# A fused H3 layer and gated product, forward and backward: the product of gate and up on GpSimd, part of the gradient turned by DMA, two buffers for k and v, paced late weights

## The chip, the cores and the metric

One core of one Trainium2 chip. The metric is the device time of one execution in microseconds (us). Every ratio below is between fast runs of the same chip and the same rounds. A time of a stage comes from one profiled run of each kernel, some of them on other chips; kernels with the same code in a stage differ there by up to some 5 us, so smaller differences of one stage are not read as effects, except where several runs agree. A ratio is the mean time of one kernel's fast runs over the mean of the other's in the same rounds, so it is not quite the ratio of the medians quoted beside it.

TensorE is PE in the profile, VectorE DVE, ScalarE ACT, GpSimd POOL, SyncE SP.

## The reference, cut to what matters

Forward pass and all gradients in bfloat16, with S = 2048 rows, D = 1024, F = 3584:

```python
xn = layernorm(q)
k_shift = causal 4-tap filter of k with shift_k;  kv = k_shift * v
y  = irfft(rfft(kv, 2S) * rfft(ssm_k, 2S))[:S] + kv * ssm_D      # long convolution
g  = xn @ w_gate;  u = xn @ w_up;  h = g * u                     # 2048 x 3584
out = q + (xn * y) * silu(h @ w_down)
# returned: out and the gradients of q, k, v, shift_k, ssm_k, ssm_D, w_gate, w_up, w_down
```

The product h = g * u is the one that the change moves. `dbm`, the gradient that flows into `h @ w_down`, is the one that it turns by DMA.

## The kernel before: the parts that the change touches

Stage one runs the projections of gate and up on TensorE in 14 slabs of 256 columns of F, and beside them, as generators that hand over in turn, the forward convolution, whose arithmetic is almost all on VectorE. `tt` is a VectorE `tensor_tensor`, `V` is `nc.vector`; `st` stores through GpSimd's DMA queue, `ld` loads or stores through SyncE's.

```python
def gu_unit(sl, b0, n, w, tick):                      # n row blocks of one slab
    gut = fg.tile([P, 4, 2, SLW], BF16, name="gut")
    hN = fg.tile([P, 4, SLW], BF16, name="hN")
    for i in range(n):
        ...                                           # 8 matmuls into ps
        nc.scalar.copy(out=gut[:, i]..., in_=ps[:])
        tick()                                        # convolution work is handed out here
    sta(GUd[...], gut[:, 0:n])
    tt(hN[:, 0:n], gut[:, 0:n, 0], gut[:, 0:n, 1], MUL)          # h on VectorE
    st(Hd[sl][:, b0:b0 + n, :], hN[:, 0:n])
    def turn():                                       # TensorE transposes of hN, some units later
        ...
    defer(turn)

# forward convolution
def load_kv(dp, c):
    v = U[4][:, 0:2048]...;  cld_v(v, c, dp * 256, 256)
    k = kst.tile([P, 2, 11, P], BF16, name="k")       # one buffer
    ...
def shift(dp):                                        # per piece: 7 products and sums, then
    ...
    st(KSHd[...], acc)
    nx = 2 * dp + c + 1                               # the next piece
    if nx < 8: load_kv(nx // 2, nx % 2)
...
w, wld = load_slab(sl, nc.sync)
if sl in (2, 4, 7):
    with tc.issue_after(wld.ins):
        copy_k({2: 1, 4: 2, 7: 3}[sl])                # k to its layout in DRAM, for the loads of k

# down product with the gate: 16 row blocks b
st(DBMd[:, b, :], dbm)
def turn():                                           # 8 transposes a block on TensorE
    ...
defer(turn)

# gradient of w_down, slab k
if k in (1, 2, 3, 4, 5): load_wgu(k - 1, ...)         # transposing loads for the last stage
if k in (6, 7, 8, 9): ts.append(load_dgut(0, k - 6))
...
ld(o_dwd[f0:f0 + P, :], wbs)
```

## Time and profile before

The time before was 2076.62 us (median of 3 runs). The stages below are cut at the first matmul of each stage in the trace of the profiled run; the last one ends with the last instruction of an engine, so they add up to the span within a few us.

| stage | us | TensorE waits most for |
|---|---|---|
| projections and forward convolution | 572.1 | hN (product on VectorE), 15.5 us |
| down product and gate | 204.8 | nothing for more than 1.1 us at a time |
| gradients of gate and up, backward convolution | 660.2 | dht (copies on ScalarE), 12.8 us; kvx, which the change is after, 4.2 us |
| gradient of w_down | 219.5 | h, 6.1 us |
| input gradient | 412.9 | dxn, 2.4 us |

### The profile page before, as it was taken

To read this page: it belongs to the slowest core of one execution; us is meant where nothing else is said; L and a number is where in the kernel's file an instruction comes from. 1 tells how busy PE (TensorE), PEld (TensorE's weight loads), DVE (VectorE), ACT (ScalarE), POOL (GpSimd) and SP (SyncE) were. 2 spreads that over 40 slices of the span, in tenths; PEclk is the share of its full clock that TensorE was granted. 3 is DMA by queue.
4 is the path that set the end of the run, shared out by engine and by line. 5 is a ranking of instruction groups with operands and counts; after the bars stand their busy time and mean duration, and the time that the engine had idled before them with its cause. 6 is when DMAs were issued, how large, how long until landed. Compare 5 with 4: busy or idle time off the path is not lost.

```text
span 2072.6 us, 29102 instructions
## 1 busy us (share of the span) xinstructions
PE 1974.6 (95%) x11626; PEld 1060.4 (51%) x11626; DVE 1488.6 (72%) x2009; ACT 617.7 (30%) x966; POOL 342.9 (17%) x499
## 2 busy tenths in 40 slices
PE   6989999999999998999898999999989999999998
PEld 3445555555544446666565555565444444444443
DVE  8689999999745556887799999989488024444343
ACT  5644544444423332222222222222122201101112
POOL 3212212221112111000122112011111101110100
PEclk9999999999999999999999999999999999999999
DMA  8675776567597869666888888668974989393921
GB/s 286 221 261 202 241 246 241 198 220 264 184 329 253 278 238 291 215 201 183 265 260 244 238 243 259 202 228 235 188 228 155 230 198 226 98 203 98 232 73 56
DMA packets 454792, 451.30 MB, mean 218 GB/s; under 512 B 237072, under 2 KB 381240, under 8 KB 440192
## 3 DMA queue, kind: packets, MB, share of 16 engines
q1 hardware_dynamic: 310320, 186.94, 35.4%
q0 software_dynamic: 45200, 189.08, 26.6%
q10 hardware_dynamic: 99136, 73.42, 11.7%
q8 instruction: 91, 1.49, 0.3%
q14 instruction: 45, 0.37, 0.1%
HBM read 208.15 MB, written 194.02 MB: 194 GB/s over the span
## 4 chain that ended last, share of the span: by engine, by line
PE 56%; DVE 19%; issue 14%; DMA 8%; POOL 2%; ACT 1%; SPq 1%; ACTq 0%; POOLq 0%; DVEq 0%
PE psx L1213 17%; PE psb L1092 10%; PE psbm L954 8%; PE psb L1190 7%; DVE W L199 5%; PE psg L553 5%; DVE m L199 5%; PE psb L1073 4%; DVE HX L199 2%; DMA B<-KFd 2%; DVE U L199 1%; DMA KSLd<-in_A_k_dram 1%; DMA B<-HFd 1%; DVE KX L199 1%; PE psY L404 1%
## 5 line engine op out<-in xcount | busy, mean ns | idle before, releaser
L553 PE MATMUL psg<-wslab,U 128*128 128x512 bf16 x1792 | 414.9, 382 | 7.1 <-ACT U L529 5.0
L1092 PE MATMUL psb<-U,U 128*128 128x512 bf16 x1792 | 396.9, 380 | 7.1 <-ACT dht L1075 3.3
L1213 PE MATMUL psx<-U,dgut 128*128 128x512 bf16 x1536 | 335.7, 379 | 2.4 <-DVE dxn L199 2.4
L1213 PEld LDWEIGHTS <-dgut 128*128 128x128 bf16 x1792 | 174.0, 98 | 213.3 <-issue 6.0
L1092 PEld LDWEIGHTS <-U 128*128 128x128 bf16 x1792 | 175.3, 98 | 209.8 <-issue 10.4
L553 PEld LDWEIGHTS <-U 128*128 128x128 bf16 x1792 | 173.6, 99 | 192.1 <-issue 7.3
L1073 PE MATMUL psb<-wdt,U 128*128 128x256 bf16 x1792 | 206.3, 276 | 10.7 <-ACT dht L1075 9.5
L1190 PE MATMUL psb<-U,U 128*128 128x512 bf16 x896 | 201.2, 386 | 10.9 <-DMA U<-Hd 6.1
L555 ACT CAST gut<-psg 128x512 bf16<-128x512 f32 x224 | 131.0, 585 | 227.6 <-PE psg L553 215.7
L1073 PEld LDWEIGHTS <-U 128*128 128x128 bf16 x1792 | 176.9, 99 | 35.7 <-issue 11.3
L954 PE MATMUL psbm<-U,ht 128*128 128x512 bf16 x784 | 171.8, 379 | 0.3 <-DMA ht<-HTd 0.3
L1096 ACT CAST wb<-psb 128x512 bf16<-128x512 f32 x112 | 65.5, 585 | 319.3 <-PE psb L1092 224.2
L199 DVE TENSOR_TENSOR m<-A,B 128x1024 bf16<-128x1024 bf16 (+1 forms) x160 | 116.7, 792 | 47.8 <-DMA B<-KFd 32.2
L1190 PEld LDWEIGHTS <-U 128*128 128x128 bf16 x896 | 88.3, 99 | 117.2 <-issue 11.7
L199 DVE TENSOR_TENSOR W<-W 128x1024 f32<-128x1024 f32 (+1 forms) x144 | 146.0, 1032 | 2.7
L199 DVE TENSOR_TENSOR dka<-dkh,Wbc 128x1024 bf16<-128x1024 bf16 x16 | 11.1, 692 | 165.8 <-DMA dkh<-DKSHd 165.8
L954 PEld LDWEIGHTS <-ht 128*128 128x128 bf16 x784 | 76.0, 98 | 89.5 <-DMA ht<-HTd 0.8
L1236 ACT ACTIVATE dx_t<-dxn 128x1024 bf16<-128x1024 f32 (+1 forms) x17 | 17.1, 1007 | 341.6 <-DVE dxn L199 290.2
L1075 ACT CAST dht<-psb 128x512 bf16<-128x512 f32 x112 | 65.2, 587 | 154.9 <-PE psb L1073 102.4
L1192 ACT CAST wbs<-psb 128x512 bf16<-128x512 f32 x56 | 32.7, 585 | 176.1 <-PE psb L1190 140.5
L199 DVE TENSOR_TENSOR W<-W,psP 128x512 f32<-128x512 f32 x128 | 80.7, 681 | 5.8 <-ACT W L229 5.8
L199 DVE TENSOR_TENSOR U<-U,dht 128x2048 bf16<-128x2048 bf16 x56 | 69.1, 1233 | 21.4 <-ACT dht L1075 21.4
(233 smaller groups left out, 2362.2 us busy)
## 6 DMA issues: line engine op xcount, KB each, us to landing
U<-GUd SPq DMA_DIRECT2D x28, 1024.0 KB, 7.5
DGd<-U ACTq DMA_DIRECT2D x56, 512.0 KB, 4.9
GUd<-gut ACTq DMA_DIRECT2D x54, 512.0 KB, 4.6
A<-DYFd POOLq DMA_DIRECT2D x16, 1024.0 KB, 8.0
U<-Hd SPq DMA_DIRECT2D x15, 1024.0 KB, 6.1
out_dram<-wb ACTq DMA_DIRECT2D x224, 64.0 KB, 3.1
Hd<-hN POOLq DMA_DIRECT2D x54, 256.0 KB, 3.5
HTd<-hT POOLq DMA_DIRECT2D x54, 256.0 KB, 3.4
```

The source lines that it names most:

```text
L199: V.tensor_tensor(o, a, b, op)
L404: nc.tensor.matmul(ps[:, i, :], TI[:, j, r, k, :], gseg(G, r, j, k), start=(n == 0), stop=(n == 3))
L553: gu_mm[0] = nc.tensor.matmul(ps[:], XNT[q][:, dc, qi * P:(qi + 1) * P], w[:, dc].rearrange("p a f -> p (a f)"), start=(dc == 0), stop=(dc ...
L555: nc.scalar.copy(out=gut[:, i].rearrange("p a f -> p (a f)"), in_=ps[:])
L954: nc.tensor.matmul(ps[:, dh * 512:(dh + 1) * 512], ht(fc)[:, i * P:(i + 1) * P], WD[fc // 4][:, fc % 4, dh * 512:(dh + 1) * 512], start=(f ...
L1073: nc.tensor.matmul(ps[:, x * SLW:(x + 1) * SLW], DBMT[2 * hf + g][:, dc, (b % 4) * P:(b % 4 + 1) * P], wdt[:, dc, :], start=(dc == 0), sto ...
L1075: nc.scalar.copy(out=dht[:, 2 * e:2 * e + 2].rearrange("p b f -> p (b f)"), in_=ps[:])
L1092: nc.tensor.matmul(ps[:], XN[b // 4][:, b % 4, dc * P:(dc + 1) * P], dgus[b // 8][:, b % 8].rearrange("p a f -> p (a f)"), start=(b == 0), ...
L1096: nc.scalar.copy(out=wb[:].rearrange("p a f -> p (a f)"), in_=ps[:])
L1190: nc.tensor.matmul(ps[:], h[:, b, f * P:(f + 1) * P], DBM[b // 4][:, b % 4, dh * 512:(dh + 1) * 512], start=(b == 0), stop=(b == NB - 1))
L1192: nc.scalar.copy(out=wbs[:, dh * 512:(dh + 1) * 512], in_=ps[:])
L1213: nc.tensor.matmul(ps[:, dh * 512:(dh + 1) * 512], t[n][:, f, i * P:(i + 1) * P], WGU[n][:, f, dh * 512:(dh + 1) * 512], start=(n == 0 and ...
```

## The change

The intent was to relieve VectorE, the second bound of stage one, of the 60 products hN, and TensorE of 96 transposes, and to take away waits for k, for kvx and for slabs of h behind late weights. The diff, cut to its core (a fixed alternation of ScalarE and VectorE for some copies in the layer norm, the order of one root, and the layout of DBMd that the transposing loads need are left out):

```diff
-    nc.vector.tensor_tensor(diag[:], ident_f[:, 0:64], ident_f[:, 64:128], ADD)      # moved later
@@ gu_unit
-        tt(hN[:, 0:n], gut[:, 0:n, 0], gut[:, 0:n, 1], MUL)
+        nc.gpsimd.tensor_tensor(hN[:, 0:n], gut[:, 0:n, 0], gut[:, 0:n, 1], MUL)
@@ load_kv, shift
-            v = U[4][:, 0:2048].rearrange("p (a x) -> p a x", a=8)
+            v = U[4][:, 2048 * c:2048 * c + 2048].rearrange("p (a x) -> p a x", a=8)
-            k = kst.tile([P, 2, 11, P], BF16, name="k")
+            k = kst.tile([P, 2, 11, P], BF16, name="k", bufs=2)
-                nx = 2 * dp + c + 1
+                nx = 2 * dp + c + 2
+        load_kv(0, 1)
@@ dy_forward: load kv before dy
@@ down product
-        defer(turn)
+        if b >= 12:
+            defer(turn)
+        if bp in (3, 5, 7):
+            q = (bp - 3) // 2
+            with tc.issue_after(ht_ld.ins):
+                nc.sync.dma_start_transpose(out=DBMT[q], in_=DBMd[512 * q:512 * q + 512, :])
@@ backward pump, two ticks later
-        bpump((bcnt[0] - 8) / (BT - 8))
+        bpump((bcnt[0] - 10) / (BT - 10))
@@ gradient of w_down
-        if k in (1, 2, 3, 4, 5):
-            load_wgu(k - 1, u8((7, 8, 9, 10, 2)[k - 1], a=4))
-        if k in (6, 7, 8, 9):
-            ts.append(load_dgut(0, k - 6))
+        with tc.issue_after(wst.ins) if k > 0 else nullcontext():
+            if k in (1, 2, 3, 4, 5):
+                load_wgu(k - 1, u8((7, 8, 9, 10, 2)[k - 1], a=4))
+            if k in (6, 7, 8, 9):
+                ts.append(load_dgut(0, k - 6))
-            ld(o_dwd[f0:f0 + P, :], wbs)
+            wst = ld(o_dwd[f0:f0 + P, :], wbs)
```

More of the change, by code (lines that the diff above doesn't have):

```diff
@@ L1 @@
-from contextlib import ExitStack
+from contextlib import ExitStack, nullcontext
 import numpy as np
@@ L92, in build_kernel @@
     DXNAd = dram.tile([P, NB, D], BF16, name="DXNAd")
-    DBMd = dram.tile([P, NB, D], BF16, name="DBMd")
+    DBMd = dram.tile([S, D], BF16, name="DBMd")
     KSHd = dram.tile([8, P, NB, P], BF16, name="KSHd")
@@ L486, in ln_load @@
         ld(x4[:, 0:n, :], xq[:, c, r0:r0 + n, :])
-    tr_ln = [None]
+    tr_ln, act_copy = [None], [None]
     def layer_norm(b0, n, x4):
@@ L503, in layer_norm @@
         r0_ = small("r0_")
-        root = nc.scalar.activation(r0_, vpe, ACT.Sqrt)
+        with tc.issue_after(act_copy[0].ins) if act_copy[0] is not None else nullcontext():
+            root = nc.scalar.activation(r0_, vpe, ACT.Sqrt)
         mean_b = small("mean_b", BF16)
@@ L528, in layer_norm @@
                 tr_ln[0] = nc.tensor.transpose(ps[:, dc, :], x4[:, i, dc * P:(dc + 1) * P], ident[:])
-            nc.any.tensor_copy(XNT[q][:, :, qi * P:(qi + 1) * P], ps[:])
+            if i % 2 == 0:
+                act_copy[0] = nc.scalar.copy(out=XNT[q][:, :, qi * P:(qi + 1) * P], in_=ps[:])
+            else:
+                V.tensor_copy(XNT[q][:, :, qi * P:(qi + 1) * P], ps[:])
         return last, root, st(XNd[:, b0:b0 + n, :], x4[:, 0:n, :])
@@ L707, in build_kernel @@
                 build_tables(ps_st, tg, ang)
+    tt(diag[:], ident_f[:, 0:64], ident_f[:, 64:128], ADD)
     for p_ in (lnp, lns, tg, bsb):
@@ L775, in load @@
         def load(ds):
+            kv = cx.tile([P, NB, P], BF16, name="kvx")
+            cld(kv[:], KVd[ds])
             x = cx.tile([P, NB, P], BF16, name="dyx")
             cld(x[:], DYd[ds])
-            kv = cx.tile([P, NB, P], BF16, name="kvx")
-            cld(kv[:], KVd[ds])
             return x, kv
@@ L979, in gate @@
         tt(dbm, dgg, sig, MUL)
-        st(DBMd[:, b, :], dbm)
+        st(DBMd[b * P:(b + 1) * P, :], dbm)
         tt(ds_t, do_t, gg, MUL)
@@ L1129, in build_kernel @@
             for q in range(4):
-                ld(DBM[q], DBMd[:, 4 * q:4 * q + 4, :])
+                ld(DBM[q], DBMd[512 * q:512 * q + 512, :].rearrange("(b u) d -> u b d", u=P))
             hs[1] = load_h(1, HSL[1])
```

## The prediction

> **What bounds the kernel now.** I read the page first, then busy time by stage, then the waits of TensorE (PE), then the timelines at the longest waits. The stages are: projections of gate and up with the forward convolution between them (60 to 575 us), the down product with the gate (575 to 776), the gradients of gate and up with the backward convolution (776 to 1437), the weight gradient of down (1437 to 1650), the input gradient (1650 to the end).
>
> ```profile
> PE   6989999999999998999898999999989999999998
> DVE  8689999999745556887799999989488024444343
> ```
>
> PE is busy nearly everywhere, VectorE (DVE) only in stage one and from 1000 to 1300 us. In us, with instruction counts in brackets, for PE, PEld, DVE, ACT and POOL:
>
> ```profile
> 60.00:575.00 515.00, 490.94 (x3048) 273.80 (x3047) 465.11 (x608) 247.43 (x386) 117.99 (x179) 0.99 0.68 232
> 1000.00:1300.00 300.00, 278.82 (x1699) 167.90 (x1698) 292.54 (x345) 71.67 (x127) 56.47 (x85) 0.98 0.83 245
> 1437.00:1650.00 213.00, 202.12 (x1032) 95.30 (x1031) 130.85 (x151) 41.97 (x75) 28.12 (x18) 0.97 0.86 203
> ```
>
> Stage one has two bounds at once: PE 491 and DVE 465 of 515 us. What PE cannot shed: 56 products of 128x512 follow each other in 12.09 us in the chain of work, 0.216 us each; 256 wide takes 0.109, 128 wide 0.056 (16 transposes 1.06 us against 8 in 0.61). 7168 x 0.216 + 2816 x 0.109 + 1120 x 0.056 and some 22 us of odd shapes make about 1940 us. So at most some 133 us of 2073 are to be had at all. The wait list of PE adds up to 88 us; its largest entries among those the change touches:
>
> ```profile
> PE tr L567 <- DVE hN L199: 15.5, 9, 6.4
> PE psb L1190 <- DMA U<-Hd: 6.1, 1, 6.1
> PE psb L1190 <- ACT wbs L1192: 4.7, 1, 4.7
> PE psY L790 <- DMA kvx<-KVd: 4.2, 1, 4.2
> ```
>
> The first is the product hN on DVE, which stands in DVE's order behind convolution work; its longest wait (108 to 114 us) comes because DVE itself stood still 10 us for a load of k. The second and third lie in the weight gradient, where the SyncE queue was held up:
>
> ```profile
> 1459.23 26.40 SPq L1149 DMA_TRANSPOSE U<-in_B_w_up_dram  x1
> 1485.72 0.53 SPq L62 DMA_DIRECT2D out_dram<-wbs  x1
> 1486.35 10.57 SPq L1149 DMA_TRANSPOSE U<-in_B_w_gate_dram  x1
> 1496.97 4.32 SPq L1155 DMA_TRANSPOSE dgut<-DGd  x2
> 1501.39 0.53 SPq L62 DMA_DIRECT2D U<-Hd  x1
> ```
>
> Transposing loads for a much later stage are issued in a row; an output store waits behind one for 26 us, and the slab of h that PE wants at 1502 us is issued only at 1501.
>
> **What the Trainium skill says.** (1) "SBUF — State Buffer", section "SBUF: two separate sides": GpSimd and DVE share a port pair, locked exclusively for a whole instruction; a DVE instruction with two SBUF inputs blocks against a GpSimd instruction that reads SBUF. The trace agrees, twice. The first two lines below are GpSimd's and DVE's own rows at one time, the last two at another:
>
> ```profile
> 1396.21 3.94 POOL L898 COPY ho<-yl 128x2048 bf16<-128x2048 bf16 x1
> 1395.91 5.39 DVE L243 SCALAR_TENSOR_TENSOR B<-W 128x512 bf16<-128x512 f32 x3
> ...
> 8.73 1.91 POOL L163 TENSOR_TENSOR m<-f,tcol 128x1024 int32<-128x1024 int32 x1
> 9.51 1.22 DVE L123 TENSOR_TENSOR diag<-ident_f 128x64 f32<-128x64 f32 x1
> ```
>
> Four instructions like the three of L243 take 2.5 us in the chain elsewhere, so three should take 1.9 and lost 3.5 us to a GpSimd copy of 3.9. The tiny diag took 1.22 us and ended 0.1 us after the GpSimd multiply. (2) "GPSIMD Engine Reference", section 3.1: about 2.6 cycles an element for two inputs[...]; the trace's only such multiply, 1024 elements, took 1.91 us, which I use. (3) "TensorE: Matmul & The Clock Gate", "What's actually happening": after an idle window of about 3.4 us PE runs at half rate. The clock record here shows it near each of the waits of 4 us and more (a granted clock of 0.93 in the window 100 to 150, 0.94 in 1450 to 1500, 0.92 in 1500 to 1550), so such a wait costs more than its length.
>
> **Part by part.**
>
> *Product on GpSimd.* 60 products leave DVE at 0.685 us; 53 of them (36 us) lie in 60 to 575. Each now takes GpSimd about 1.9 us and, by (1), locks DVE out for most of it. DVE is nearly always at work there, mostly with two SBUF inputs; only the sums with a PSUM input (87 of 465 us) go on. 52 x 1.85 us x 0.85 gives 82 us lost against 36 saved. Beside that DVE is idle 46 us in this stretch, of which some 28 us before its convolution work ends: 17 for k, 11 for gut in front of hN. I let 20 of them go. The convolution thus ends about 82 - 36 - 20 = 26 us later. The projections' last tenth of work stands after it in PE's order, so **stage one becomes some 26 us longer**. PE's 15.5 us of waits for hN mostly go, but turn into waits for convolution results (psY on HX, psP on W), since DVE now sets the pace.
>
> *Two buffers for k and v.* The loads are issued one piece ahead; the 10 us idle of DVE at 99 us and 7 us of smaller ones go. That is in the 20 above.
>
> *Layer norm order, diag moved.* diag stood 1.2 us in DVE's first, critical chain; the copies alternate between ScalarE and DVE by rule. **-1 us.**
>
> *Gradient turned by DMA.* 12 of 16 blocks lose 8 transposes each: 96 x 0.056 = **-5.4 us** of PE, in a stage where PE runs without gaps. In their place come three transposing loads of 1 MB, some 5 us each on the SyncE queue[...] (L1149's median is 4.6 to 5.1), at DMA load 0.84. Each reads rows stored two pairs of blocks, 25 us or more, before, and the loads of the next h have some 17 us of slack: free. The last four blocks stay on PE because they would come too late.
>
> *kv before dy, pump two ticks later.* kvx was issued 0.54 us after dyx and came last; PE waited 4.3 us, then 2.7 us for the first sums, and half clock cost 1.7 us. kvx now is loaded first, and the first products stand two ticks (some 3 us) later. **-5.5 us**, and perhaps **-3** where DVE lags at 1000 to 1300.
>
> *Paced late weights.* Each transposing load stands after the stores of the slab before, one in 13.8 us, and the next slab of h stands ahead of it. Waits of 4.9 and 6.3 us at 1491 and 1502 go, and two half-clock stretches, which held some 4.75 and 5.9 us of work at half rate, 5.3 us. Of these 16.5 I take **-13**, for one slow transpose (26 us) may still hold up a store. The input gradient starts without a wait on its weights now, and its last loads depend on buffers that are freed no earlier: no change.
>
> Sum: +26 - 1 - 5.4 - 5.5 - 3 - 13 = -2 us: 2075.
>
> **The rivals.** *The lock is cheap.* If GpSimd only fills DVE's pauses, or its multiply of bf16 is much shorter than 1.9 us, DVE keeps the 36 us and the 20 us. Then the waits of stage one (24 us from 100 to 575, and 5 us of half clock) nearly vanish: -27 there, -28 elsewhere, 2022. For it: diag is moved away from the GpSimd multiply, so the clash seems to have been seen, and the product was moved all the same. Against it: both overlaps above, one of them with a multiply. I give it 0.3. *GpSimd's queue becomes the bound.* It issues stores in order, and HTd stores wait for ScalarE, KFd and HFd stores for DVE (29 and 15 us in all). A product behind such a store comes late, PE's transposes with it, and PE then feeds DVE late. The order of instructions puts most products before the KFd and HFd stores, so it adds 10 to 20 us at most: 2085 to 2095. I give it 0.2. *Transposes crowd the DMA* in the down product, and h comes late: +5 to +10 us; 0.1, because h is fetched a pair of blocks ahead.
>
> **Range and chances.** My sum is 2075; the first rival pulls to 2022, the second to 2090. The weighted middle is 2066, nearer my sum. Eight times in ten: 2024 to 2094. Faster by 2% means under 2035, which needs the lock to cost almost nothing: 0.22. Slower by 2% means over 2118, which needs both bad rivals: 0.04. Within 2%: 0.74.
>
> **What would show it.** Stage one: DVE busy near 100% with its two-input rows longer in the mean, hN rows on POOL at about 2 us, and waits of PE for HX and W in place of hN; end of the projections near 600 us against 575. If the multiply takes 1 us, or DVE's rows keep their lengths, that step is wrong. No wait for k of 10 us. L993 with 32 transposes, the down product shorter by 5 us. No PE wait on kvx. Transposes of the late weights some 14 us apart, and no PE wait on Hd or wbs. If these last still stand, the pacing was not the cause; if dgut or the weights appear as waits of psx, it came at a price.

## The result, and the profile after

The changed kernel takes **2173.09 us** (2172.44 to 2182.11, 4 runs); the kernel before took 2073.44 us (2051.54 to 2078.22, 4 runs) on the same chip. The ratio is 1.0512, with a 95% interval of 1.0431 to 1.0593: slower by 5%. It is correct.

| stage, us | before | after | difference | predicted |
|---|---|---|---|---|
| projections and forward convolution | 572.1 | 690.3 | +118.2 | +25 |
| down product and gate | 204.8 | 199.2 | -5.6 | -5.4 |
| gradients of gate and up | 660.2 | 658.3 | -1.9 | -8.5 |
| gradient of w_down | 219.5 | 203.1 | -16.4 | -13 |
| input gradient | 412.9 | 418.3 | +5.4 | 0 |

The loss lies in stage one; the +5.4 us of the last stage is taken up in the section on the prediction. The busy rows of the page of the changed kernel, in 40 slices of 54 us:

```profile
PE   6979676876898999899999899999999999998998
DVE  7788699688783555488879989999879204434433
POOL 4464655556544221100011211201110101111100
PEclk9999898898999999999999999999999999999999
```

Stage one is the first 13 slices. TensorE has holes there that it did not have before, and its granted clock drops with them. VectorE does not run at its limit either: it has holes too (busy 533 of 690 us, against 511 of 572 before). So neither engine is busy throughout; both wait for something else. The waits of TensorE, then one of VectorE's, in us in total, times, longest:

```profile
PE tr L570 <- POOL hN L562: 110.2, 12, 22.8
```

```profile
DVE U L198 <- DMA KSHd<-U: 41.8, 3, 20.9
```

The wait for hN, 15.5 us before, is 110.2 us now. The tile view of hN, before and after, with the shortest, the median and the longest duration in ns:

```profile
L199 DVE TENSOR_TENSOR hN<-gut x60: 284/685/693, 17.1 to 570.9; 128x1024 bf16<-128x1024 bf16 x54, 128x256 bf16<-128x256 bf16 x4, 128x512 bf16<-128x512 bf16 x2
```

```profile
L562 POOL TENSOR_TENSOR hN<-gut x60: 661/2129/22914, 16.3 to 687.6; 128x1024 bf16<-128x1024 bf16 x54, 128x256 bf16<-128x256 bf16 x4, 128x512 bf16<-128x512 bf16 x2
```

The median is what the prediction said, some 2 us. But eight of the 60 took 11 to 23 us for the same work. One of them in GpSimd's timeline (start, duration):

```profile
215.85 0.72 POOL L65 DMA_DIRECT2D HTd<-hT  x1
216.58 22.91 POOL L562 TENSOR_TENSOR hN<-gut 128x1024 bf16<-128x1024 bf16 x1
239.79 0.58 POOL L65 DMA_DIRECT2D Hd<-hN  x1 [0.30 <-POOL hN L562]
```

and VectorE's timeline beside it, with the cut lines all of the same kind, without a pause between them:

```profile
220.28 3.62 DVE L198 TENSOR_TENSOR m<-KX,HX 128x2048 bf16<-128x2048 bf16 x5
...
226.23 1.21 DVE L198 TENSOR_TENSOR U<-k,Wbc 128x2048 bf16<-128x2048 bf16 x1
...
236.31 1.21 DVE L198 TENSOR_TENSOR U<-U 128x2048 bf16<-128x2048 bf16 x1
237.56 3.02 DVE L198 TENSOR_TENSOR U<-k,Wbc 128x2048 bf16<-128x2048 bf16 x1
```

From 216.58 to 237.5 us VectorE runs 24 instructions (the one at hand at 216.58 included), each at its normal length (1.21 us for the U at 226). Then the U at 237.56 takes 3.02 us, 1.8 us too long, and GpSimd's product ends 1.94 us after that U began. So GpSimd's instruction had begun by its record but stood still inside for 20.8 us, until it got in; then VectorE stood still for it. The instruction before which it got in is also the first that waited for the one right ahead of it: U was written at 236.31 to 237.52, and the next began 35 ns after that end, where the others begin some 77 ns before the end of the one ahead.

The stores and loads on GpSimd's queue stand behind such an instruction as well. That is the wait of 41.8 us above: VectorE wants the buffer U, whose store KSHd was not yet issued. In the longest of these waits the store was issued at 406.96 us. The long product had ended at 385.9; between the two, GpSimd's queue worked off in order what stood ahead of the store, three stores of HTd that waited for ScalarE and two more products that waited for gut.

Elsewhere the change did what it should. SyncE's queue in the gradient of w_down after the change (start, duration):

```profile
1562.76 6.74 SPq L1159 DMA_TRANSPOSE U<-in_B_w_gate_dram  x1
1576.91 0.33 SPq L62 DMA_DIRECT2D U<-Hd  x1
1577.91 10.25 SPq L1159 DMA_TRANSPOSE U<-in_B_w_up_dram  x1
```

One transposing load for each slab, some 15 us apart, with the slab of h between them; no wait of TensorE for h or for wbs is left.

### The profile page after: what moved, and what is told of

Same layout as the page of the kernel before. It is cut to its first block, busy times and chain, and to the rows that moved or that the text cites. A ratio compares the mean times of both kernels' runs of the same rounds, so it can differ in the third digit from the quotient of the medians.

```text
span 2171.9 us, 28682 instructions
## 1 busy us (share of the span) xinstructions
PE 1976.3 (91%) x11346; PEld 1061.9 (49%) x11530; DVE 1512.9 (70%) x1947; ACT 607.3 (28%) x956; POOL 586.7 (27%) x559
## 4 chain that ended last, share of the span: by engine, by line
PE 60%; DVE 12%; issue 10%; POOL 10%; DMA 6%; ACT 1%; SPq 0%; ACTq 0%; POOLq 0%; DVEq 0%
PE psx L1224 17%; PE psg L556 9%; PE psb L1201 9%; PE psb L1102 8%; PE psbm L959 8%; POOL hN L562 8%; DVE W L198 3%; DVE m L198 3%; PE psb L1083 3%; DVE U L198 1%; DMA B<-HFd 1%; PE tr L570 1%; PE psP L215 1%; DMA dyl<-DYd 1%; PE psS L215 1%
## 5 line engine op out<-in xcount | busy, mean ns | idle before, releaser
L556 PE MATMUL psg<-wslab,U 128*128 128x512 bf16 x1732 | 424.2, 393 | 10.4 <-ACT U L530 4.3
L1102 PE MATMUL psb<-U,U 128*128 128x512 bf16 x1745 | 397.3, 382 | 8.8 <-ACT wb L1106 2.5
L562 POOL TENSOR_TENSOR hN<-gut 128x1024 bf16<-128x1024 bf16 (+2 forms) x60 | 245.4, 4091 | 44.9 <-ACT gut L558 40.6
L1201 PE MATMUL psb<-U,U 128*128 128x512 bf16 x876 | 194.8, 379 | 1.1
L1083 PEld LDWEIGHTS <-U 128*128 128x128 bf16 x1792 | 176.5, 99 | 38.4 <-issue 14.5
L570 PE MATMUL tr<-ident,hN 128*128 128x128 bf16 x448 | 38.7, 233 | 111.5 <-POOL hN L562 110.2
L198 DVE TENSOR_TENSOR dka<-dkh,Wbc 128x1024 bf16<-128x1024 bf16 x16 | 11.1, 692 | 173.9 <-DMA dkh<-DKSHd 173.9
L1247 ACT ACTIVATE dx_t<-dxn 128x1024 bf16<-128x1024 f32 (+1 forms) x17 | 17.1, 1007 | 346.8 <-DVE dxn L198 293.5
```

The costliest lines, as they stand in the source:

```text
L198: V.tensor_tensor(o, a, b, op)
L556: gu_mm[0] = nc.tensor.matmul(ps[:], XNT[q][:, dc, qi * P:(qi + 1) * P], w[:, dc].rearrange("p a f -> p (a f)"), start=(dc == 0), stop=(dc ...
L562: nc.gpsimd.tensor_tensor(hN[:, 0:n], gut[:, 0:n, 0], gut[:, 0:n, 1], MUL)
L570: nc.tensor.transpose(ps[:, a, i, :], hN[:, i, a * P:(a + 1) * P], ident[:])
L1083: nc.tensor.matmul(ps[:, x * SLW:(x + 1) * SLW], DBMT[2 * hf + g][:, dc, (b % 4) * P:(b % 4 + 1) * P], wdt[:, dc, :], start=(dc == 0), sto ...
L1102: nc.tensor.matmul(ps[:], XN[b // 4][:, b % 4, dc * P:(dc + 1) * P], dgus[b // 8][:, b % 8].rearrange("p a f -> p (a f)"), start=(b == 0), ...
```

## The experiments

### First: which part, and of what nature

Four kernels ran together with the one before (2064.18 us, median of 7 runs). The edits, in order:

```diff
# e1_product_dve: the changed kernel with
-        nc.gpsimd.tensor_tensor(hN[:, 0:n], gut[:, 0:n, 0], gut[:, 0:n, 1], MUL)
+        tt(hN[:, 0:n], gut[:, 0:n, 0], gut[:, 0:n, 1], MUL)
# e2_product_pool_alone: the kernel before with the opposite edit, nothing else
# e3_pauses: the changed kernel with 72 pauses in the forward convolution, of this form
# (what follows a pause is also held to stay behind it)
+            behind[0] = V.tensor_copy(gapt[:], m2[:, 0, 1, 0, 0:1])    # reads what was just written
+            with tc.issue_after(behind[0].ins): ...                    # the next products
# e4_pool_memset: the changed kernel with (wrong on purpose)
-        nc.gpsimd.tensor_tensor(hN[:, 0:n], gut[:, 0:n, 0], gut[:, 0:n, 1], MUL)
+        nc.gpsimd.memset(hN[:, 0:n], 0.03125)
```

> The changed kernel with the product hN back on VectorE, all else as changed. Theory (GpSimd's product is kept waiting inside the instruction while VectorE runs two-input instructions without a pause, and PE waits for hN): the 110 us of PE waits for hN from GpSimd go, the projections end at 570 us or earlier instead of 690, the other stages keep their 19 us gain: 2030 to 2055 us. Rival (the other edits of stage one, layer norm order or the two buffers, cost the 118 us): stays above 2120 us.

> The kernel before with the product hN on GpSimd and nothing else changed. Theory: the projections alone grow by 100 to 130 us, the other stages stay within 5 us each: 2175 to 2205 us, slower than the changed kernel itself. Rival (other edits at fault): within 30 us of before.

> The changed kernel, product on GpSimd, with a one-column VectorE copy after each group of the frequency product and inverse transform that waits for the instruction just ahead, so that VectorE drains there (some 9 a channel block, 0.2 us each, 15 us of VectorE in all). Theory of starvation: GpSimd gets in at each pause, no product takes over 8 us (23 in the changed kernel), PE waits for hN fall from 110 to under 35 us: 2085 to 2125 us. Rival A (VectorE loses 2 us to each product and is the bound): unchanged or up to 15 us slower than the changed kernel. Rival B (the product stands behind stores in GpSimd's queue): unchanged within 10 us.

> Wrong result on purpose: in the place of the product GpSimd fills hN with a constant, same count, same place in its queue, reading no SBUF and not waiting for gut. Theory (contention for the SBUF read side): each fill takes under 1.5 us, none over 4, PE waits for hN under 10 us, time 2020 to 2055 us. Rival B (queue order behind stores that wait for ScalarE and VectorE): PE still waits 50 us or more for hN, over 2100 us.

| kernel | median us | ratio to before (95%) | stage one us | VectorE busy there | hN longest us | TensorE waits for hN us |
|---|---|---|---|---|---|---|
| before (profiled first) | | | 572.1 | 510.7 | 0.69 | 15.5 |
| after | 2173.09 | 1.0512 (1.0431 to 1.0593) | 690.3 | 533.0 | 22.91 | 110.2 |
| e1, product back on VectorE | 2053.47 | 0.9942 (0.9895 to 0.9989) | 577.5 | 510.2 | 0.69 | 19.0 |
| e2, product on GpSimd alone | 2181.16 | 1.0559 (1.0502 to 1.0615) | 691.5 | 535.4 | 22.92 | 103.3 |
| e3, pauses | 2115.28 | 1.0238 (1.0190 to 1.0285) | 636.0 | 558.7 | 7.77 | 23.1 |
| e4, memset (2 runs) | 2049.83 | 0.9920 (0.9851 to 0.9989) | 570.3 | 477.6 | 1.08 | none |

What follows:

- **The product on GpSimd is the whole loss.** Alone it makes stage one 691.5 us; without it the rest of the change leaves 577.5. e1 is faster than the kernel before, if by little (0.6%). Two details missed their expectation: stage one of e1 was to end at 570 us or earlier, and e2's other stages were to stay within 5 us, but its gradient of w_down took 210.3 us instead of 219.5.
- **The long waits are a loss of their own.** Pauses on VectorE, which only add work to it, make the changed kernel some 57 us faster (1.0238 against 1.0512 of the kernel before), because GpSimd now gets in (longest 7.77 us instead of 22.91):

```profile
L583 POOL TENSOR_TENSOR hN<-gut x60: 660/2224/7773, 16.2 to 633.4; 128x1024 bf16<-128x1024 bf16 x54, 128x256 bf16<-128x256 bf16 x4, 128x512 bf16<-128x512 bf16 x2
```

- **What is left can be accounted for by VectorE's own loss.** With the pauses, stage one is still 58.5 us longer than in e1. VectorE's instructions other than hN and the pauses keep it busy 556.0 us in stage one, where e1 with its products is busy 510.2: +45.8 us. The pauses cost some 0.18 us each (measured in the isolated run below: the next product began 0.78 us after the one ahead instead of 0.60), so 72 x 0.18 = 13 us. That makes 59 of the 58.5. This is a sum of busy times, not a run with that loss alone; the third experiment gives one.
- **Little was to be won by this step alone.** With a GpSimd instruction that reads no SBUF, VectorE is relieved of the products for nothing (its other instructions take 477.6 us, 479.2 in e1), and stage one is 570.3 us, 7 less than e1 and 2 less than before. VectorE is idle 93 us instead of 67 there; 14.7 us of it are the wait for k that the fourth experiment removes. A free product together with that repair was not run.

### Second: the lock alone

My theory by then: GpSimd gets in only where VectorE drains. Its rival was the prediction's picture, in which it gets in when the instruction at hand ends. The kernel runs only this (its outputs are zero): in each of eight cases, 14 VectorE instructions and one GpSimd instruction that may start after the second.

```python
for k in range(14):
    with tc.issue_after(last.ins):
        last = nc.vector.tensor_tensor(o[k], a, b, MUL)        # A: independent, 128x1024 bf16
    if k == 1:
        nc.gpsimd.tensor_tensor(h, o[1], b, MUL)
# B: a pause after the seventh; C: each reads the one ahead; D: f32; E: one input in PSUM;
# F: multiply by a number; I, J: GpSimd copies, or multiplies by a number
```

> A measurement by itself, its outputs zero on purpose. Each case has 14 VectorE instructions and one GpSimd instruction that is free to start after the second of them. Theory (the two engines exclude each other, and GpSimd gets in only where VectorE drains): A, independent two-input bf16 products of 0.6 us, GpSimd two-input: GpSimd's lasts until the run of VectorE is over, about 9 us, and no VectorE instruction is lengthened. B, the same with a small copy after the seventh that waits for the seventh: GpSimd starts there, about 5 us, and the next VectorE instruction lasts some 2.6 us. C, each VectorE instruction reads what the one ahead wrote: GpSimd gets in at once, 2.1 to 2.8 us, and one VectorE instruction grows by some 2.1 us. D, f32 products 512 wide: as A, 8 us or more. E, VectorE reads PSUM: neither is lengthened, GpSimd about 1.1 us. F, VectorE with one SBUF input (multiply by a number): open[...]. I and J, GpSimd copy and GpSimd multiply by a number beside A's run: open; as A if any GpSimd access is excluded. Rival (GpSimd gets in at the next instruction's end, as my prediction had it): A to D all about 2.1 to 2.8 us for GpSimd, with one VectorE instruction lengthened by about 2.1 us each.

GpSimd's timeline, cases A, C, E and F (start, duration):

```profile
6.33 2.49 POOL L86 TENSOR_TENSOR hA<-Ax,b 128x1024 bf16<-128x1024 bf16 x1 [5.91 <-DVE Ax L81]
...
27.83 2.62 POOL L86 TENSOR_TENSOR hC<-Cx,b 128x1024 bf16<-128x1024 bf16 x1 [8.41 <-DVE Cx L85]
...
49.52 1.27 POOL L92 TENSOR_TENSOR hE<-Ex,bf 128x512 bf16<-128x512 f32 x1 [8.09 <-DVE Ex L84]
57.62 2.23 POOL L86 TENSOR_TENSOR hF<-Fx,b 128x1024 bf16<-128x1024 bf16 x1 [6.83 <-DVE Fx L82]
```

A drain is a place where a VectorE instruction starts only after the one ahead has ended. Each case of this run and of the next stands in one execution alone.

**My expectation failed:** in case A GpSimd got in at once, without any drain; the fourth VectorE instruction took 2.60 instead of 0.68 us. B (2.50 us), D (1.65) and the other kinds of GpSimd instruction, I (1.43) and J (3.14), got in at once as well. So being back to back is not enough to keep GpSimd out. What the run did show: the exclusion itself holds against two SBUF inputs and against a multiply of one by a number (F: one of those instructions took 2.34 instead of 0.42 us), and not against a PSUM input (E: all 0.68 us). Beside I and J, whose GpSimd instruction has one input, the lengthened VectorE instruction took 1.52 us.

I then went back to the trace of the changed kernel and counted, for each product of GpSimd that found VectorE busy, how many VectorE instructions had run since its last drain or PSUM input. Those that got in at the next boundary had mostly 0 to 3; of the eight long waits, six had 4 to 10. That gave the next run: the same, with 28 products a case, and GpSimd released after the 2nd, 4th, 6th, 9th or 14th; with the 9th also a PSUM operation (P9) or a dependent copy (D9) after the 18th.

```diff
-            if k == 1:
+            if k == at:                       # at = 2, 4, 6, 9, 14
+            if k == 18 and kind == "psum":  last = V.tensor_tensor(fl[:], af[:], pin[:], MUL)
+            if k == 18 and kind == "drain": last = V.tensor_copy(key[:], t[:, 0:1])
```

> A second measurement by itself, outputs zero on purpose. In the first one GpSimd was released after the second VectorE product of a run and was let in at the next boundary in every case, against my theory that a run without a gap keeps it out. In the changed kernel itself it is let in at the next boundary where at most some 3 products have run since VectorE last drained or read PSUM, and mostly kept out where more have. Here a run of 28 products of 0.6 us, GpSimd released after the 2nd, 4th, 6th, 9th and 14th. Theory (VectorE claims the port ahead once it has run some products without a drain): after the 2nd as before, 2.5 us; after the 9th and 14th it lasts until the run is over, about 13 and 10 us; after the 4th and 6th either, and that places the threshold. With an operation that reads PSUM after the 18th (release after the 9th) and with a small dependent copy there: about 8 us, let in there. Rival (what keeps GpSimd out is something in the kernel's own instructions, not the length of the run): 2.1 to 2.8 us in all seven.

```profile
6.13 2.49 POOL L71 TENSOR_TENSOR hA<-A2x,b 128x1024 bf16<-128x1024 bf16 x1 [5.69 <-DVE A2x L68]
26.36 2.50 POOL L71 TENSOR_TENSOR hA<-A4x,b 128x1024 bf16<-128x1024 bf16 x1 [17.73 <-DVE A4x L68]
46.60 15.14 POOL L71 TENSOR_TENSOR hA<-A6x,b 128x1024 bf16<-128x1024 bf16 x1 [17.74 <-DVE A6x L68]
67.61 13.33 POOL L71 TENSOR_TENSOR hA<-A9x,b 128x1024 bf16<-128x1024 bf16 x1 [5.87 <-DVE A9x L68]
89.82 10.32 POOL L71 TENSOR_TENSOR hA<-A14x,b 128x1024 bf16<-128x1024 bf16 x1 [8.88 <-DVE A14x L68]
106.02 7.31 POOL L71 TENSOR_TENSOR hP<-P9x,b 128x1024 bf16<-128x1024 bf16 x1 [5.88 <-DVE P9x L68]
125.05 7.31 POOL L71 TENSOR_TENSOR hD<-D9x,b 128x1024 bf16<-128x1024 bf16 x1 [11.72 <-DVE D9x L68]
```

VectorE's timeline of the case A6, behind the release:

```profile
46.43 13.33 DVE L68 TENSOR_TENSOR A<-a,b 128x1024 bf16<-128x1024 bf16 x22
61.77 0.16 DVE L80 COPY fA<-hA 128x1 bf16<-128x1 bf16 x1 [2.00 <-POOL hA L71]
```

Here is the mechanism by itself. Released after the 2nd or 4th product, GpSimd gets in at the next boundary and takes 2.5 us. Released after the 6th or later, it is kept out until the whole run is over: the 22 products behind it take 13.33 us, 0.60 each, not one of them lengthened, and only then does GpSimd work, while VectorE waits 2.00 us for it. A PSUM operation or a dependent copy after the 18th lets it in there (7.31 us). The theory holds in a corrected form: **what keeps GpSimd out is a gapless run of VectorE instructions that was already some five long when GpSimd asked.** Why five is not shown; that VectorE's queue has by then claimed the port ahead is my reading, not a measurement. Nor is it shown that a count decides: all products here are alike, 0.60 us apart, so a time between 2.4 and 3.6 us would fit as well. And the count does not explain every case in the kernel: two of its eight long waits (at 145 and 443 us) began one product after an instruction with a PSUM input, with 15 or 16 instructions since GpSimd had last got in, while others in that position (at 133 and 430 us) got in at the next boundary.

### Third: VectorE's loss without a late hN

```diff
# e10_product_twice: e8 below (product on VectorE, one buffer for k and v), and
+        with tc.issue_after(made.ins):                      # made: hN on VectorE
+            nc.gpsimd.tensor_tensor(idle_[:, 0:n], <constant>, <constant>, MUL)   # nobody reads idle_
```

> The changed kernel with hN's product on VectorE and one buffer for k and v (as run before: 577 us in the projections, 2056 us), and behind each product an unused product of the same size on GpSimd, of a constant tile into a scratch tile. Nothing waits for the scratch, so hN is never late. Theory of two parts (late hN, and VectorE held up while GpSimd has the port): only the second part remains; the projections take 577 + 45 to 75 us, the time is 2100 to 2130 us, the waits of TensorE for hN stay under 35 us. Rival (only the late hN and the late queue cost): 575 to 590 us in the projections, time at most 2070 us. If GpSimd's stores queued behind the long instructions are late, a wait of VectorE for a store shows it and is to be taken off.

It ran in 2118.36 us (ratio 1.0253, 1.0225 to 1.0281), and stage one took 639.3 us against 577.3 in e8: +62.0, inside the expectation. VectorE was busy 587.8 against 509.9 us: +78 us for 60 products. One thing was not as I had written it: the unused products did not stay behind their hN but ran ahead, nearly back to back, and were over at 202 us, so the loss fell in the first third of the stage. It is a clean price for the lock, not a copy of the changed kernel. None of these products was kept out for long, at most some 0.9 us. That agrees with the runs above: these products came so close, each stopping VectorE, that no run of it grew long.

### Fourth: the other parts, each undone on top of e1

```diff
# e5_k_early: the second copy of k right behind the first, not in slab 2
     copy_k(0)
+    copy_k(1)
# e6_no_pacing: late weights issued as before
-        with tc.issue_after(wst.ins) if k > 0 else nullcontext():
+        if True:
# e7_turn_pe: all 16 blocks of the gradient turned on TensorE
-        if b >= 12:
-            defer(turn)
+        defer(turn)
# e8_one_buffer: load_kv and shift as before the change
```

> Product on VectorE as in e1, and the second copy of k from its input to its slab in DRAM issued right behind the first, at about 20 us, and no longer behind the weights of slab 2 at 88 us. Theory (VectorE's 11 us of idle time at 101 us waits for that copy, and the two buffers of k and v cannot help): the idle time and PE's 9.8 us wait for hN at 108 us go, the projections end some 10 us earlier than e1's 577.5 us: ratio to before near 0.989. Rival (the buffer or the load itself is the cause): no change from e1, ratio 0.994.

> Product on VectorE as in e1, late weights not paced. If the pacing alone won the 16.5 us of the down-weight gradient: that stage is back to 215 to 222 us from 203.1, all others as in e1: ratio to before near 1.002. If the gain came from elsewhere (another alignment of the convolution): stage stays within 5 us of 203.

> Product on VectorE as in e1, all 16 blocks of the down gradient turned on PE again. By the step of 96 transposes at 0.056 us: the down product takes 204 to 205 us instead of 198.9, the other stages within 2 us: ratio to before near 0.997.

> Product on VectorE as in e1, one buffer for k and v again. If the two buffers win nothing because the wait is for the copy in DRAM: projections within 3 us of e1's 577.5. If they are worth something: 5 us or more longer.

The kernel before took 2070.01 us (median of 11) on this chip.

| kernel | median us | ratio to before (95%) | stage it concerns |
|---|---|---|---|
| e5, k early | 2051.14 | 0.9919 (0.9884 to 0.9955) | projections 569.5 (e1: 577.5) |
| e6, no pacing | 2066.61 | 0.9990 (0.9959 to 1.0021) | gradient of w_down 210.7 (203.1) |
| e7, turned on TensorE | 2073.43 | 1.0022 (0.9984 to 1.0061) | down product 205.0 (198.9) |
| e8, one buffer | 2056.32 | 0.9934 (0.9906 to 0.9963) | projections 577.3 (577.5) |

**Two buffers win no time:** e8 is as fast as e1. They do take some shorter waits for k away (19.3 us in 5 waits in e8, 11.1 in one in e1), but these ended nothing. The long wait that they were meant for is still in e1, on VectorE:

```profile
DVE U L198 <- DMA k<-KSLd: 11.1, 1, 11.1
```

It is for data, not for a buffer: k comes from a copy within DRAM that stands in SyncE's queue behind the weights of slab 2. e5 issues the copy early; the wait is gone and stage one is 8 us shorter, as expected, though the ratio (0.9919) stays within the interval of e1's.

**Pacing works, at about half the expected size.** Without it (e6) a transposing load holds up SyncE's queue again and the slab of h is late by 5.4 us. The stage took 210.7 us, though, where 215 to 222 were expected; in e2, which has no pacing either, it took 210.3. So pacing is worth some 7 us there. The 219.5 us of the kernel before stand in one profile alone; what the other 9 were is not shown.

```profile
1463.75 21.06 SPq L1159 DMA_TRANSPOSE U<-in_B_w_gate_dram  x1
```

**The gradient by DMA** is worth 6.1 us in its stage (205.0 against 198.9). The rest of e7's time is not this, and the other stages did not stay within the expected 2 us: in its profiled run the stage after it has a hole, where the issue of two output stores on ScalarE's queue took 22.44 us. Its runs spread from 2063 to 2083 us, so it may be common in that kernel; I did not find its cause, and it stays open.

### Last: are the remaining waits for hN worth anything?

```diff
# e11_k_early_prio: e5, and
+        with tc.high_priority(40):
             tt(hN[:, 0:n], gut[:, 0:n, 0], gut[:, 0:n, 1], MUL)
```

> The best version so far (product on VectorE, k's second copy early: 2051 us) with hN's product placed about 40 places earlier in VectorE's order. TensorE still waits 10 to 19 us for hN in these versions. If those waits end last: up to 10 us less, most likely 3 to 5, so 2044 to 2050 us. If what follows hN then is late in its place (the DFT chain): 2051 us or a little more. Memory of the chip is used as before.

It took 2047.50 us (2043.29 to 2053.24, 6 runs) beside 2068.35 us of the kernel before, ratio 0.9907 (0.9881 to 0.9933): inside e5's interval. The time alone does not decide, since it also lies in the range that was expected if these waits had ended last. TensorE's waits in e11:

```profile
PE psY L403 <- DVE HX L198: 8.1, 8, 1.6
PE tr L571 <- DVE hN L198: 2.5, 2, 1.4
```

In e5 they were 3.3 us for HX and 11.4 us for hN. So hN earlier made HX later, and stage one is 571.1 instead of 569.5 us. Ending the waits for hN thus shows no gain in stage one. e5 and e11 are the fastest correct versions here, some 1% below the kernel before; between them there is no measured difference.

## Why the prediction was wrong

It said 2066 us, 2024 to 2094, and 0.74 for within 2%; the time was 2173.09. Of the steps:

- **Product on GpSimd: wrong, and the whole of the miss.** The prediction's term was "82 us lost against 36 saved", less 20 us of VectorE's idle time, so that "stage one becomes some 26 us longer". It became 118 longer, 113 of which come from the product (690.3 against 577.5 in e1). The three parts of that term:
  - *The loss under the lock was sized right for a GpSimd that gets in soon.* In e3 VectorE's instructions without hN and pauses grew from 479.2 us (e1) to 556.0, by 77 us; in e10 VectorE's busy time grew by 78; the term said 82. In the changed kernel itself they grew less, to 533.0 us, by 54.
  - *The 20 us of idle time to be won back did not come:* two buffers win no time (e8), and even a free product gains only 7 us (e4).
  - *The step that failed is the wait: it left out the other direction of the lock.* It let VectorE wait for GpSimd but took each product to be done in GpSimd's 1.9 us as soon as gut was there. In fact GpSimd is kept out by runs of VectorE, up to 20.8 us at a time. In the changed kernel's own trace VectorE is busy 23 us more than in e1 (533.0 against 510.2) and idle 90 us more (157.2 against 67.3): the idle time, which the term wanted to shrink by 20 us, is most of the 113. With it come the late hN (110.2 us of TensorE's waits), half clock on TensorE (119.5 us of stage one after, 17.1 in e1, 68.3 in e3) and the stores of KSHd behind it (41.8 us of VectorE's waits). e3 shows the same from the other side: it takes 54 us from the stage in spite of its pauses' 13. No kernel had the late hN without VectorE's loss, so the two are told apart by busy and idle time and by e10, not by a run of each.
- **The rival "GpSimd's queue becomes the bound"** was close in kind, with products late and TensorE late with them, but its reason was the queue's order, and its size 10 to 20 us. Order did play a part, behind the long products: two waits of VectorE for KSHd took 19.7 and 20.9 us. The prediction's sign for "TensorE's 15.5 us of waits for hN mostly go" was wrong: they became 110.2.
- **The rival "the lock is cheap"** fell twice: the lock isn't cheap, and even where it is avoided (e4) stage one gains 7 us, not 27.
- **Two buffers for k and v: wrong for the long wait.** The 10 us at 99 us were read as a wait for a buffer one piece ahead; e8 and e5 show that it is one for the copy in DRAM. The smaller waits went as predicted (19.3 us in e8, 11.1 in e1), without a gain in time.
- **Layer norm order, diag: -1 us, not shown.** Stage one of e1 is 5.4 us longer than before, and e6 and e8 agree with e1 (577.4 and 577.3), but only one profile of the kernel before stands against them; e5 gets 8 us back, but from another wait. No run undid this part alone.
- **Gradient by DMA: right.** -5.4 us predicted, -5.6 measured from before to after, 6.1 in e7 against e1; no TensorE wait for the turned blocks.
- **kv before dy and the later pump: right on the wait, the gain not shown.** The wait for kvx went from 4.2 us to under 1.1, but the stage gained 1.9 us, not 8.5, and that is within what the stage varies: e2, with the old order and a wait for kvx of 4.1 us, took 655.8 us there, less than the changed kernel's 658.3. TensorE's waits for dht there stayed (12.8 us before, 14.5 after). No run tested this part alone, so a gain is not shown.
- **Paced late weights: right in kind, too large in size.** -13 predicted, -16.4 measured in the stage from before to after; but undoing it alone costs 7.6 us there, and e2, unpaced too, took 210.3 us. That the predicted and the measured total lie close is partly luck.
- **Input gradient: 0 predicted, +5.4 measured.** The changed kernel has a wait for dxn of 5.9 us, which e1, with the same code there, doesn't have (410.4 us). It varies between kernels; I leave it open.
- **The weighted middle** of 2066 us is not quite what its own chances give (0.3 x 2022 + 0.2 x 2090 + 0.5 x 2075 = 2062); nothing turns on it.

From the Trainium skill, the prediction took that the loser of the shared port "fully blocks" ("SBUF — State Buffer", section "SBUF: two separate sides"), but applied it to VectorE as the only loser. The same passage says that whichever engine starts first has the pair, so GpSimd can be the loser too. Read both ways, it would have led to the question how long VectorE goes without a gap: here 24 instructions beside one of the longest waits. That count stood in the trace before: a timeline of VectorE in the convolution shows its products one behind another.

## What to carry to other kernels

Before moving an elementwise product to GpSimd to relieve a busy VectorE, ask both questions: what does VectorE lose while GpSimd has the port (here 1.3 us for each 0.6 us saved), and how long a gapless run of VectorE can keep GpSimd out, with whoever needs the result and everything on GpSimd's queue behind it. If it must be there, give VectorE a dependent instruction every few instructions, as e3 did; one with a PSUM input let GpSimd in too in the isolated run, but two long waits of the kernel began one product after such an instruction; if VectorE is nearly full, leave it where it is. And ask of a wait for a load whether it is for the buffer or for the data: only the first is helped by a second buffer.

## What the Trainium skill lacked or had wrong

- "SBUF — State Buffer", section "SBUF: two separate sides": it says that the pair is held for one instruction. It lacks that the wait of a blocked GpSimd instruction is not bounded by one instruction of VectorE: released after the 6th product of a gapless run, it waited for all 22 that followed (15.14 us for 2.1 us of work), and after the 4th for less than one (2.50 us). It also lacks what lets GpSimd in: a dependent instruction or one with a PSUM input (7.31 us instead of 13.33). On which VectorE instructions count, the runs agree with it that two SBUF inputs block (0.68 to 2.60 us); one input in PSUM did not (0.68 us throughout). A multiply of one SBUF input by a number blocked too (0.42 to 2.34 us); the section counts such an instruction only in a two-port mode, and no run here shows the mode.
- "GPSIMD Engine Reference", section 3.1: some 2.6 cycles an element for two inputs. In the kernel an undisturbed product of 1024 elements took 2.11 us, 2.06 ns each, so this agrees within some 7% with an estimate of 2.2 ns worked out from it and the page's clock. The duration of a GpSimd row in the profile includes the time in which it is locked out; no page that I read names this (22.91 us for the same product).
- No page that I read tells that pauses can pay: 72 small dependent copies on VectorE, which cost some 13 us, made the changed kernel some 57 us faster.
